# Packed 64-bit integer adds for GpSimd's tile shifts in a fused attention kernel

## Chip, cores, metric

One core of one Trainium2 chip. The metric is the device time of one execution in microseconds; a quoted time is the median of a kernel's runs. "Span" is the length of the one profiled execution, some 2 us less than a timed one. Ratios to the kernel before are the mean time of one kernel's fast runs over that of the other's of the same rounds, so not quite the ratio of the medians that are quoted.

## The reference

Two attention-like layers on separate inputs, whose outputs are put side by side. The change concerns the first, softmax attention with 32 heads of 16 over 2048 positions and one shared key and value head:

```python
def _A_ref(x, wq, wk, wv, wo):
    q = (x @ wq).reshape(B, S, 32, 16).transpose(0, 2, 1, 3)
    k = x @ wk
    v = x @ wv
    p = softmax(einsum("bhqd,bkd->bhqk", q, k) * 0.25)
    o = einsum("bhqk,bkd->bhqd", p, v)
    return o.transpose(0, 2, 1, 3).reshape(B, S, 512) @ wo
# B: linear attention with softmax feature maps, 32 heads; out = concat([A, B], -1)
```

## The kernel before

A Python scheduler inside the kernel plans the whole program with durations from its author (a "job" has an engine and a duration), and emits a fixed order for every engine. No order is decided at run time. The exponentials of the scores are shared out. ACT computes some with its Exp function into PT. DVE makes others: one linear map of a score tile to int16 (line 1743), whose bits, read as fp16, approximate an exponential. Four such tiles with bits offset by 0, 256, 512 and 768 form the terms of the approximation, and PE sums them with four scaled copies of V (VK, line 1811). A "quad" is four score tiles (128x2048) and its three offset copies; the ring Z has 12 slots of this size.

The offset copies, called shifts, are made by DVE or GpSimd ("pool"):

```python
def shifts(self, quad):
    ...
            if eng == "dve":
                fn = lambda v: v.tensor_scalar(out=Z[:, z], in0=Z[:, z0], scalar1=256.0 * t, ...)   # L1769
            else:
                a, b = (Z[:, x].rearrange("p h n -> p (h n)").bitcast(I32) for x in (z0, z))
                c = self.step[:, t - 2, :].bitcast(I32).to_broadcast([128, 1024])
                fn = lambda g: g.tensor_tensor(out=b, in0=a, in1=c, op=ALU.add)                     # L1774
    ...
    for t in (3, 2, 1):          # who makes shift t: GpSimd if its planned backlog allows
        left = max(self.te["pool"] - self.fin, 0.0) + self.PSHIFT * self.pooled
        eng = "pool" if t > 1 and left < self.PLEFT[3 - t] else "dve"
```

Shift 1 is always DVE's, and the program lets a GpSimd shift wait by semaphore for the DVE shifts of its own quad (cut from the code above: `deps=own`).

GpSimd also multiplies each of the first 31 of 32 finished accumulator blocks by the reciprocal of its denominators, and does small work for the linear attention:

```python
def finish_sc3(self, sc):        # L1879, 31 times
    self.add("pool", lambda v: v.tensor_tensor(out=o, in0=accS[:, r, :], in1=R[:, r, :], op=ALU.mult), ...)
def b_bm(self, st):              # L2080, 16 times, 128x64
    self.add("pool", lambda g: g.tensor_tensor(out=bmx, in0=ssum[:, r, :], in1=bmx, op=ALU.add), ...)
def b_kvfin(self):               # L2139 to L2144, once: 9 tensor_tensor, 1 tensor_scalar
```

## Time and profile before

| | before |
|---|---|
| time | 733.73 us (733.67 to 736.96, 3 runs) |
| PE, DVE, ACT, GpSimd busy, of a span of 731.1 us | 95%, 94%, 97%, 60% |
| shifts on GpSimd / DVE | 197 / 247 |
| mean GpSimd shift | 1893 ns |
| PE's wait for GpSimd's Z tiles | 1.5 us |

"Busy" is the time in which an engine executes something. ACT, PE and DVE are each close to full, so a gain has to lighten all three; GpSimd is the only one with room. The last row says that today its tiles are always ready in time. The lines themselves stand in the prediction.

### The profile page before, as it was taken

To read this page: it belongs to the slowest core of one execution; us is meant where nothing else is said; L and a number is where in the kernel's file an instruction comes from. 1 tells how busy PE (TensorE), PEld (TensorE's weight loads), DVE (VectorE), ACT (ScalarE), POOL (GpSimd) and SP (SyncE) were. 2 spreads that over 40 slices of the span, in tenths; PEclk is the share of its full clock that TensorE was granted. 3 is DMA by queue.
4 is the path that set the end of the run, shared out by engine and by line. 5 is a ranking of instruction groups with operands and counts; after the bars stand their busy time and mean duration, and the time that the engine had idled before them with its cause. 6 is when DMAs were issued, how large, how long until landed. Compare 5 with 4: busy or idle time off the path is not lost.

```text
span 731.1 us, 17986 instructions
## 1 busy us (share of the span) xinstructions
PE 693.6 (95%) x7450; PEld 215.9 (30%) x7450; DVE 686.1 (94%) x1157; ACT 709.5 (97%) x799; POOL 438.6 (60%) x307
## 2 busy tenths in 40 slices
PE   9999899999999999999999999999999999999995
PEld 3222222223222323322333323333333332332221
DVE  4899999999999999998999999999999999999991
ACT  5999999999999999999999999999999999999995
POOL 4474456666677566676346764455677556576553
PEclk9999999999999999999999999999999999999999
DMA  7620233111012110111101111101111012121002
GB/s 146 117 37 7 39 37 77 9 10 12 5 10 38 11 11 3 13 8 9 12 11 13 23 27 24 15 7 17 17 26 23 13 16 34 24 31 13 6 9 41
DMA packets 47890, 18.28 MB, mean 25 GB/s; under 512 B 38708, under 2 KB 45940, under 8 KB 47800
## 3 DMA queue, kind: packets, MB, share of 16 engines
q1 hardware_dynamic: 45400, 16.23, 17.5%
q8 instruction: 60, 0.98, 0.5%
q10 hardware_dynamic: 2400, 0.82, 0.5%
q14 instruction: 30, 0.25, 0.1%
HBM read 2.28 MB, written 4.19 MB: 9 GB/s over the span
## 4 chain that ended last, share of the span: by engine, by line
ACT 43%; PE 34%; DVE 19%; DMA 1%; POOL 1%; issue 0%; SPq 0%; ACTq 0%
ACT f_PT L1644 42%; PE f_ps L1589 12%; DVE f_Z L1743 10%; PE f_ps L1811 9%; DVE f_Z L1769 5%; PE f_ps L1685 4%; PE f_ps L2246 2%; PE f_ps L2154 1%; PE f_ps L1579 1%; PE f_ps L1898 1%; ACT f_Ek L2064 1%; DVE f_Wk L2216 1%; DMA f_AxT<-in_A_x_dram 1%; PE f_ps L2056 1%; PE f_ps L2230 1%; PE f_ps L2172 1%
## 5 line engine op out<-in xcount | busy, mean ns | idle before, releaser
L1644 ACT ACTIVATE f_PT<-f_ps 128x1024 bf16<-128x1024 f32 x728 | 680.7, 1076 | 11.8 <-PE f_ps L1589 10.8
L1774 POOL TENSOR_TENSOR f_Z<-f_Z,f_step 128x1024 int32<-128x1024 int32 x197 | 373.0, 1893 | 264.9 <-DVE f_Z L1769 258.9
L1743 DVE TENSOR_SCALAR f_Z<-f_ps 128x512 int16<-128x512 f32 x592 | 379.8, 679 | 13.0 <-PE f_ps L1589 11.7
L1589 PE MATMUL f_ps<-f_QA,f_KR 32*128 32x512 bf16 x2048 | 295.8, 384 | 21.1 <-ACT f_PT L1644 17.1
L1811 PE MATMUL f_ps<-f_Z,f_VK 128*32 128x512 f16 x2368 | 211.9, 386 | 5.7 <-POOL f_Z L1774 1.5
L1769 DVE TENSOR_SCALAR f_Z<-f_Z 128x2048 int16<-128x2048 int16 x247 | 168.0, 706 | 0.0
L1589 PEld LDWEIGHTS f_ps<-f_QA,f_KR 32*128 32x128 bf16 x2048 | 74.0, 91 | 260.9 <-ACT f_PT L1644 229.0
L1685 PE MATMUL f_ps<-f_PT,f_VA 128*32 128x512 bf16 x1456 | 137.4, 385 | 0.2
L1811 PEld LDWEIGHTS f_ps<-f_Z,f_VK 128*32 128x32 bf16 x2368 | 52.3, 93 | 109.2 <-issue 56.3
L1685 PEld LDWEIGHTS f_ps<-f_PT,f_VA 128*32 128x32 bf16 x1456 | 35.8, 94 | 49.1 <-issue 44.2
L1408 PE MATMUL f_ps<-f_ones,f_zero 128*128 128x512 bf16 (+5 forms) x182 | 34.5, 346 | 1.6 <-POOL f_zero L1427 1.3
L2216 DVE TENSOR_TENSOR f_Wk<-f_ps,f_wq 128x512 bf16<-128x512 f32 x32 | 21.8, 681 | 0.4 <-PE f_ps L2205 0.3
L1879 POOL TENSOR_TENSOR f_On<-f_accS,f_denS 128x512 bf16<-128x512 f32 x16 | 20.6, 1286 | 2.6 <-POOL f_Z L1774 0.4
L1414 DVE COPY f_accS<-f_ps 128x512 f32<-128x512 f32 x31 | 21.0, 679 | 0.0
L1879 POOL TENSOR_TENSOR f_Ot<-f_accS,f_denS 128x512 bf16<-128x512 f32 x15 | 19.0, 1269 | 3.1 <-DMA f_denS<-f_denS 1.3
L2104 DVE TENSOR_TENSOR f_vS<-f_ps,f_rs 128x1024 bf16<-128x1024 f32 x16 | 19.4, 1211 | 0.3 <-PE f_ps L2094 0.2
L2070 DVE TENSOR_REDUCE f_ssum<-f_Ek 128x64 f32<-128x1024 bf16 x16 | 19.2, 1200 | 0.0
L2064 ACT ACTIVATE f_Ek<-f_ps 128x512 bf16<-128x512 f32 x32 | 18.6, 681 | 0.0
L2161 ACT ACTIVATE f_ET<-f_ps 128x512 bf16<-128x512 f32 x32 | 18.5, 672 | 0.0
L2246 PE MATMUL f_ps<-f_Bwo,f_oT 128*128 128x512 bf16 x64 | 16.6, 382 | 0.6 <-DVE f_Z L1743 0.6
L1579 PE MATMUL f_ps<-f_AxT,f_wq 128*128 128x512 bf16 x64 | 16.4, 381 | 0.2 <-DVE f_Z L1743 0.2
L2094 PE MATMUL f_ps<-f_Bwv,f_BxT 128*128 128x512 bf16 x64 | 16.6, 382 | 0.0
(96 smaller groups left out, 303.1 us busy)
## 6 DMA issues: line engine op xcount, KB each, us to landing
f_denS<-f_denS SPq DMA_DIRECT2D x124, 30.0 KB, 3.1
out_dram<-f_outB SPq DMA_DIRECT2D x16, 128.0 KB, 1.9
f_denC<-f_accS SPq DMA_DIRECT2D x124, 2.0 KB, 1.7
f_denS<-f_denC SPq DMA_DIRECT2D x124, 2.0 KB, 1.7
out_dram<-f_outA SPq DMA_DIRECT2D x14, 128.0 KB, 1.9
f_On<-f_Ot SPq DMA_DIRECT2D x60, 16.0 KB, 1.8
f_Bwv<-in_B_wqkv_dram SPq DMA_DIRECT2D x1, 512.0 KB, 6.0
f_Bwo<-in_B_wo_dram SPq DMA_DIRECT2D x1, 512.0 KB, 4.5
```

Source lines behind the costliest of these rows:

```text
L1408: mm = pe.matmul(ps[m * i:m * i + m, bank, 0:n].rearrange("p (a n) -> p a n", n=128), lhsT=zero[0:r, 0:m], rhs=rhs, start=start, stop=star ...
L1589: return pe.matmul(self.ps[:, bank, :], lhsT=self.KR[32 * g:32 * g + 32, sc % 2, kap * 128:(kap + 1) * 128], rhs=self.QA[32 * g:32 * g + 3 ...
L1644: self.add("act", lambda a: a.activation(out=PT[:, sl[0]:sl[0] + size, :], in_=ps[:, b0:b0 + size, :], func=ACT.Exp), reads=[("PS", b0 + i ...
L1685: mm = pe.matmul(ps[32 * g:32 * g + 32, bank, :], lhsT=VA[:, kap, :], rhs=PT[:, slots[g], :], start=start, stop=stop, tile_position=(0, 32 ...
L1743: self.add("dve", lambda v: v.tensor_scalar(out=o, in0=ps[:, bank, :], scalar1=self.Z1, scalar2=self.Z0, op0=ALU.mult, op1=ALU.add), reads ...
L1769: fn = lambda v: v.tensor_scalar(out=Z[:, z], in0=Z[:, z0], scalar1=256.0 * t, scalar2=None, op0=ALU.add)
L1774: fn = lambda g: g.tensor_tensor(out=b, in0=a, in1=c, op=ALU.add)
L1811: mm = pe.matmul(ps[32 * g:32 * g + 32, bank, :], lhsT=self.VK[:, t, kap, :], rhs=Zf[:, sl[g], :], start=start, stop=stop, tile_position=( ...
L1879: self.add("pool", lambda v: v.tensor_tensor(out=o, in0=accS[:, r, :], in1=R[:, r, :], op=ALU.mult), reads=[("accS", r), ("denS", r), ("ro ...
L2064: self.add("act", (lambda a, sg: (lambda e: e.activation(out=Ek[:, r, a, :, :], in_=ps[:, bank, :].rearrange("p (h f) -> p h f", h=32), fu ...
L2216: self.add("dve", lambda v: v.tensor_tensor(out=o, in0=i, in1=w.unsqueeze(3).to_broadcast([128, 2, 16, 16]), op=ALU.mult), reads=[("PS", b ...
L2246: mm = pe.matmul(ps[:, bank, :], lhsT=oT[:, r, C, :], rhs=self.Bwo[:, C, :], start=(C == 0), stop=(C == 3))
```

## The change

The intent: an add of 32-bit words with a second input stream becomes an add of 64-bit words with an immediate, four int16 lanes a word (the bits are such that no lane overflows). One input stream in place of two should halve the time of a shift, and the scheduler, told 1.1 us in place of 1.97, should give GpSimd more of them.

```diff
+I64 = mybir.dt.int64
...
-                    a, b = (Z[:, x].rearrange("p h n -> p (h n)").bitcast(I32) for x in (z0, z))
-                    c = self.step[:, t - 2, :].bitcast(I32).to_broadcast([128, 1024])
-                    fn = lambda g: g.tensor_tensor(out=b, in0=a, in1=c, op=ALU.add)
+                    a, b = (Z[:, x].rearrange("p h n -> p (h n)").bitcast(I64) for x in (z0, z))
+                    fn = lambda g: g.int64_add(out=b, in0=a, in1=256 * t * 0x1000100010001)
...
-    PSHIFT = 1.97
+    PSHIFT = 1.1
```

## The prediction

> **What bounds the kernel now.** I read the page's first two parts first, to see whether any engine stands out. None does: three engines are near full, and GpSimd (POOL) is the one with room.
>
> ```profile
> PE 693.6 (95%) x7450; PEld 215.9 (30%) x7450; DVE 686.1 (94%) x1157; ACT 709.5 (97%) x799; POOL 438.6 (60%) x307
> ```
>
> Then the chain that ended last, by engine: it hops between ACT, PE and DVE all through the span, and GpSimd carries 1% of it.
>
> ```profile
> ACT 43%; PE 34%; DVE 19%; DMA 1%; POOL 1%; issue 0%; SPq 0%; ACTq 0%
> ```
>
> So the kernel is a balanced static schedule. It splits the attention scores between ACT (true exponentials) and DVE, which makes one fp16 bit pattern per score tile (line 1743). The other three tiles of a quad are that tile plus 256, 512 or 768: DVE and GpSimd make these "shifts". The costliest groups name all the pieces:
>
> ```profile
> L1644 ACT ACTIVATE f_PT<-f_ps 128x1024 bf16<-128x1024 f32 x728 | 680.7, 1076 | 11.8 <-PE f_ps L1589 10.8
> L1774 POOL TENSOR_TENSOR f_Z<-f_Z,f_step 128x1024 int32<-128x1024 int32 x197 | 373.0, 1893 | 264.9 <-DVE f_Z L1769 258.9
> L1743 DVE TENSOR_SCALAR f_Z<-f_ps 128x512 int16<-128x512 f32 x592 | 379.8, 679 | 13.0 <-PE f_ps L1589 11.7
> ...
> L1811 PE MATMUL f_ps<-f_Z,f_VK 128*32 128x512 f16 x2368 | 211.9, 386 | 5.7 <-POOL f_Z L1774 1.5
> L1769 DVE TENSOR_SCALAR f_Z<-f_Z 128x2048 int16<-128x2048 int16 x247 | 168.0, 706 | 0.0
> ...
> L1879 POOL TENSOR_TENSOR f_On<-f_accS,f_denS 128x512 bf16<-128x512 f32 x16 | 20.6, 1286 | 2.6 <-POOL f_Z L1774 0.4
> ```
>
> There are 592/4 = 148 quads, and 444 shifts: 247 on DVE, 197 on GpSimd. GpSimd's 264.9 us of idleness costs nothing today, because PE waits for its tiles only 1.5 us. Last I read the timeline of GpSimd, for the rhythm of its work:
>
> ```profile
> 50.23 3.86 POOL L1774 TENSOR_TENSOR f_Z<-f_Z,f_step 128x1024 int32<-128x1024 int32 x2 [1.10 <-DVE f_Z L1769]
> 54.23 1.53 POOL L1879 TENSOR_TENSOR f_On<-f_accS,f_denS 128x512 bf16<-128x512 f32 x1
> 56.52 1.89 POOL L1774 TENSOR_TENSOR f_Z<-f_Z,f_step 128x1024 int32<-128x1024 int32 x1 [0.75 <-DVE f_Z L1769]
> ```
>
> Shifts are broken by one floating-point multiply (line 1879) for each of 31 accumulator blocks. The first multiply starts at 54.2 us and the last at 719.0, so the rhythm is (719.0 - 54.2)/30 = 22.2 us a block, and 12.1 us follow the last one.
>
> **What the Trainium skill says.** "GPSIMD Engine Reference", section Performance versus the Vector engine: an add with two inputs is bound by two reads that take turns on one port, a body with at most two operations by about one cycle an element. The trace agrees: the two-input add of 1024 words takes 1893 ns, the fill of 1024 words of f_denS, with no input, 951 ns. The same page, section Instruction dispatch: GpSimd kernels are loadable libraries, and the first call after a load costs about 6 us (5.95 measured there), with no instruction visible in the profile. No view of the kernel before shows this cost: its fast path holds one library selection, of the library that is resident anyway, between the fills of f_half and the TENSOR_SCALAR after them, and the gap is an ordinary 0.09 us. "SBUF — State Buffer", section on the shared port pair: a DVE instruction in a 2-port mode and a GpSimd instruction exclude each other for their whole length. The 258.9 us that line 1774 waited for DVE's line 1769 fit this, mixed with plain data waits.
>
> **The change part by part.** I set the instruction order of the built kernel after against that of before.
>
> 1. The shift itself. One input stream and an immediate instead of two streams. Estimate: the kernel's constant went from 1.97 to 1.1 and the trace's spacing of two adjacent shifts is 3.86/2 = 1.93, so 1.1/1.97 x 1.93 = 1.08; the fill at 0.95 is a floor. I take 1.05 us.
>
> 2. The new split. The scheduler now believes in cheap GpSimd shifts: 310 shifts there (197 before), 158 on DVE (247), 156 quads (592 to 624 tiles of line 1743), 712 exponentials (728). DVE: +32 x 0.679 - 89 x 0.706 = -41 us. ACT: -16 x 680.7/728 = -15 us. PE: 128 more matmuls of line 1811, 32 fewer of line 1685, at about 0.09 us of busy time each (211.9/2368) some +8 us, partly taken back by fewer filler matmuls. If nothing else changed, ACT at 97% would set the end: 731 - 15 = 716 us in the profile, about 718 timed. That is the intended gain, 2%.
>
> 3. What the diff does not show. The 64-bit add is not in the resident library; the multiply of line 1879, the sum of line 2080 and other TENSOR_TENSOR are in it and not in the other. The build therefore puts a library selection in front of each change of kind. In the main path of the built kernel I count 40 in front of shifts, 28 in front of line 1879 and 12 in front of line 2080: 80 true changes, where there was none. At 6 us (the skill's figure, my estimate for both directions) that is 80 x 6 = 480 us of GpSimd time.
>
> 4. GpSimd's sum. 310 x 1.05 = 326, other work 438.6 - 373.0 = 66, loads 480: 872 us, against a span of 731. GpSimd becomes the bound.
>
> 5. By blocks, since the loads are not spread evenly. Of 31 blocks, 24 hold one pair of loads, 5 hold two and 2 hold three (the linear-attention part's small sums split them between 100 and 330 us). A block with one pair: 9.6 shifts x 1.05 + multiply 1.3 + 2 x 6 + small work 0.5 = 24 us, just above the rhythm of 22.2. Two pairs: 11 x 1.05 + 1.3 + 24 + 1 = 38. Three: 9.5 x 1.05 + 1.3 + 36 + 1.6 = 49. Sum: first block to its multiply 58 (54.2 and some), 23 x 24 = 552, 5 x 38 = 190, 2 x 49 = 98, tail 12: 910 us. PE, DVE and ACT follow, because the order on PE is fixed: a matmul of line 1811 whose tile is late stops all behind it. The Z ring has 12 slots, three quads, so while GpSimd loads for 6 to 13 us little can be made ahead, and after a load GpSimd sometimes waits for DVE in turn. I add 20 us for this: 930.
>
> **Rivals.** (a) The loads are cheap, under 0.5 us, or hidden in GpSimd's idle time. Without loads GpSimd would be busy 326 + 66 = 392 of about 716 us, so 80 loads of up to 324/80 = 4 us would fit on average. For it: the one selection in the trace of before costs nothing. Against it: that one selects the resident library, and idle time comes in pieces of 0.6 to 2.4 us in the timeline, so even 3 us would show at the small sums. Time: 716 to 735. (b) Loads cost 3.5 to 4 us: only the 7 blocks with several pairs are bound. With 4: 23 x 22.2 = 511, 5 x 30, 2 x 37, 70: 805, and 825 with the same allowance. (c) Loads cost 8 us or the add takes 1.5: with 8, 23 x 28 + 5 x 46 + 2 x 61 + 70 = 1066, or 1086 with the allowance; with a slow add, 310 x 0.45 = 140 us on top of 930. (d) The port becomes the bound: DVE's 158 shifts at 0.71 and GpSimd's 326 us exclude each other, 438 us of 731 against 168 + 373 = 541 before, so it eases; I drop it.
>
> **Range and chances.** The mechanism, a bound GpSimd, I hold for nearly sure; the size rests on the cost of a load, which no trace of before shows, at 80 us of span for each microsecond. A cost of 3.7 to 8.7 us gives about 800 to 1140 us, and I widen below for loads partly hidden. Predicted 930 us, 8 in 10 between 790 and 1140. Faster by over 2% needs loads of nearly nothing and all of the 2% gain: 0.05. Same: 0.06. Slower: 0.89.
>
> **What would show it.** Right: GpSimd shifts start to start about 1.05 us apart in runs of several; gaps of 5 to 7 us at each change between line 1774 and lines 1879 or 2080, put down to "issue" or to nothing; PE's waits at line 1811 for GpSimd's Z tiles from 1.5 us to over 100; slices between 100 and 330 us stretched most; PE, ACT and DVE down to 75% or so; ACT's time per exponential unchanged. Wrong: gaps at the changes under 1 us (rival a); shifts of 1.5 us or more; waits of PE for DVE or ACT in place of GpSimd; or a granted clock that falls as PE idles, which would add to my time.

## The result, and the profile after

1074.14 us (1068.88 to 1078.5, 4 runs), correct; the ratio to before is 1.462 (95% interval 1.454 to 1.470). The granted clock of PE fell from 0.998 to 0.824.

The page of the kernel after: its busy line, the slices of PE and of its clock, the chain that ended last by engine, and the groups that answer to those shown of before (count | busy us, mean ns | idle before them and its main releaser).

```profile
PE 767.0 (72%) x7468; PEld 218.2 (20%) x7526; DVE 674.0 (63%) x1100; ACT 711.4 (66%) x783; POOL 392.8 (37%) x420
...
PE   8976676676265778635746687888778877997676
...
PEclk9988876688686878666858898888888898898888
...
PE 33%; issue 27%; DVE 23%; POOL 10%; ACT 3%; DMA 1%; SPq 1%; POOLq 0%; ACTq 0%; DVEq 0%
...
L1645 ACT ACTIVATE f_PT<-f_ps 128x1024 bf16<-128x1024 f32 x712 | 681.1, 1049 | 341.5 <-PE f_ps L1590 338.8
...
L1774 POOL INT64_ADD f_Z<-f_Z x310 | 327.2, 1055 | 378.1 <-issue 186.4
L1811 PE MATMUL f_ps<-f_Z,f_VK 128*32 128x512 f16 x2496 | 251.6, 447 | 219.1 <-POOL f_Z L1774 217.8
...
L1879 POOL TENSOR_TENSOR f_On<-f_accS,f_denS 128x512 bf16<-128x512 f32 x16 | 20.6, 1286 | 111.0 <-issue 111.0
```

All four engines are less full than before, GpSimd's busy share too: 37% after 60%. An eye on busy shares alone would find no bottleneck here. The chain shows it: 27% of the span is "issue", time in which the engine on the chain waited for nothing that the profile shows. The shift itself is as fast as hoped, 1055 ns for 1893. But "issue" idle time now stands in front of the shifts (186.4 us) and of the multiplies (111.0 in this row, 84.4 in the other half of them), and PE's wait at line 1811 for GpSimd's tiles went from 1.5 us to 217.8.

What the "issue" time is, shows in the trace when one asks for everything that line 1879 and line 1774 put on GpSimd's queue. The first numbers are durations in ns (least, median, most):

```profile
L1879 POOLq MODIFY_POOL_CONFIG  x56: 11/11/12, 54.8 to 1050.1; - x56
...
L1774 POOLq MODIFY_POOL_CONFIG  x80: 1/1/13, 12.4 to 1034.2; - x80
```

Two records belong to one library selection: 28 in front of multiplies, 40 in front of shifts, and (24 records at line 2080) 12 in front of the small sum. That is the count of 80 which the prediction took from the built program. The records themselves last some nanoseconds; the time follows them. One change and its return, in the timeline of GpSimd (start, duration, operation, in brackets the idle time before it):

```profile
82.15 1.04 POOL L1774 INT64_ADD f_Z<-f_Z  x1 [1.30 <-DVE f_Z L1770]
90.58 1.26 POOL L1879 TENSOR_TENSOR f_Ot<-f_accS,f_denS 128x512 bf16<-128x512 f32 x1 [7.39 <-issue]
97.66 1.03 POOL L1774 INT64_ADD f_Z<-f_Z  x1 [5.83 <-issue]
98.86 1.04 POOL L1774 INT64_ADD f_Z<-f_Z  x1 [0.17 <-POOL f_Z L1774]
```

and the chain that ended last through the same 20 us, with PE after the long wait:

```profile
83.20 0.01 POOLq L1879
...
83.25 7.33 issue
90.58 1.26 POOL f_Ot L1879
...
92.08 5.59 issue
97.66 1.04 POOL f_Z L1774
98.70 0.04 issue
98.75 1.05 PE f_ps L1811 x8
```

GpSimd makes no tile from 83.19 to 97.66, 14.5 us for one multiply of 1.26. PE's eight matmuls at 98.75 had waited 7.9 us for the tile of 97.66. Before that it had run on with earlier tiles for 7.7 us, from 83.19 to 90.85; that first part of the outage was hidden. Over the trace, the gap in front of a return to the library of the multiplies is 6.92 us in the median (6.64 to 7.67, 40 gaps, 279.4 us), in front of a change to the 64-bit library 5.82 us (5.52 to 6.03, 39 gaps, 227.5 us; the 40th lay in idle time at the start). Together 506.8 us, 6.4 us a load. The profile puts 65 of the 79 gaps down to "issue"; the other 14 name DVE or PE but are as long.

### The profile page after: what moved, and what is told of

The parts are those of the page before. It is cut to its first block, busy times and chain, and to the rows that moved or that the text cites. A ratio compares the mean times of both kernels' runs of the same rounds, so it can differ in the third digit from the quotient of the medians.

```text
span 1070.3 us, 18343 instructions
## 1 busy us (share of the span) xinstructions
PE 767.0 (72%) x7468; PEld 218.2 (20%) x7526; DVE 674.0 (63%) x1100; ACT 711.4 (66%) x783; POOL 392.8 (37%) x420
## 4 chain that ended last, share of the span: by engine, by line
PE 33%; issue 27%; DVE 23%; POOL 10%; ACT 3%; DMA 1%; SPq 1%; POOLq 0%; ACTq 0%; DVEq 0%
DVE f_Z L1744 12%; PE f_ps L1590 11%; PE f_ps L1811 11%; POOL f_Z L1774 7%; PE f_ps L1686 5%; DVE f_Z L1770 4%; ACT f_PT L1645 3%; DVE f_vS L2104 1%; DVE f_Wk L2216 1%; POOL f_On L1879 1%; DVE f_ssum L2070 1%; DVE f_accS L1415 1%; PE f_ps L2154 1%; POOL f_Ot L1879 1%; PE f_ps L2094 1%
## 5 line engine op out<-in xcount | busy, mean ns | idle before, releaser
L1645 ACT ACTIVATE f_PT<-f_ps 128x1024 bf16<-128x1024 f32 x712 | 681.1, 1049 | 341.5 <-PE f_ps L1590 338.8
L1744 DVE TENSOR_SCALAR f_Z<-f_ps 128x512 int16<-128x512 f32 x624 | 409.7, 683 | 245.0 <-PE f_ps L1590 242.9
L1774 POOL INT64_ADD f_Z<-f_Z x310 | 327.2, 1055 | 378.1 <-issue 186.4
L1811 PE MATMUL f_ps<-f_Z,f_VK 128*32 128x512 f16 x2496 | 251.6, 447 | 219.1 <-POOL f_Z L1774 217.8
L1590 PE MATMUL f_ps<-f_QA,f_KR 32*128 32x512 bf16 x2048 | 312.8, 424 | 20.1 <-ACT f_PT L1645 11.8
L1686 PE MATMUL f_ps<-f_PT,f_VA 128*32 128x512 bf16 x1424 | 149.4, 424 | 0.1
L1770 DVE TENSOR_SCALAR f_Z<-f_Z 128x2048 int16<-128x2048 int16 x158 | 118.9, 754 | 1.9 <-PE f_ps L1811 0.7
L1879 POOL TENSOR_TENSOR f_On<-f_accS,f_denS 128x512 bf16<-128x512 f32 x16 | 20.6, 1286 | 111.0 <-issue 111.0
L1879 POOL TENSOR_TENSOR f_Ot<-f_accS,f_denS 128x512 bf16<-128x512 f32 x15 | 18.9, 1261 | 84.8 <-issue 84.4
L1409 PE MATMUL f_ps<-f_ones,f_zero 128*32 128x512 bf16 (+6 forms) x162 | 31.1, 383 | 1.6 <-POOL f_zero L1428 1.3
L1844 DVE RECIPROCAL f_denC<-f_denC 128x16 f32<-128x16 f32 x31 | 7.6, 244 | 35.9 <-DMA f_denC<-f_accS 35.9
L2117 PE MATMUL f_ps<-f_vS,f_Ek 128*32 128x34 bf16 x512 | 6.6, 186 | 30.3 <-POOL f_vS L2085 30.3
L2130 DVE TENSOR_TENSOR f_kvS<-f_ps,f_kvS 128x272 f32<-128x272 f32 x15 | 6.5, 437 | 22.7 <-PE f_ps L2117 22.6
```

The lines of the kernel that those rows point to most:

```text
L1409: mm = pe.matmul(ps[m * i:m * i + m, bank, 0:n].rearrange("p (a n) -> p a n", n=128), lhsT=zero[0:r, 0:m], rhs=rhs, start=start, stop=star ...
L1590: return pe.matmul(self.ps[:, bank, :], lhsT=self.KR[32 * g:32 * g + 32, sc % 2, kap * 128:(kap + 1) * 128], rhs=self.QA[32 * g:32 * g + 3 ...
L1645: self.add("act", lambda a: a.activation(out=PT[:, sl[0]:sl[0] + size, :], in_=ps[:, b0:b0 + size, :], func=ACT.Exp), reads=[("PS", b0 + i ...
L1686: mm = pe.matmul(ps[32 * g:32 * g + 32, bank, :], lhsT=VA[:, kap, :], rhs=PT[:, slots[g], :], start=start, stop=stop, tile_position=(0, 32 ...
L1744: self.add("dve", lambda v: v.tensor_scalar(out=o, in0=ps[:, bank, :], scalar1=self.Z1, scalar2=self.Z0, op0=ALU.mult, op1=ALU.add), reads ...
L1774: fn = lambda g: g.int64_add(out=b, in0=a, in1=256 * t * 0x1000100010001)
```

## The experiments

Three theories. **LT**: the loads make GpSimd's sum of work the bound; this is step 4 of the prediction, which its step 5 takes block by block. **LS**: every pair of loads is an outage that stalls the fixed order on PE by most of its length, whatever GpSimd's sum. **P**: not the loads but the 64-bit add or the new split does it, through the port that DVE and GpSimd share. Times of each experiment are beside runs of the kernel before on the same chip; its medians there were 733.56, 735.46 and 733.97 us in the three sessions.

### No library change, same order (a wrong result on purpose)

```diff
-  op of L1879: tensor_tensor(out=o, in0=accS[:, r, :], in1=R[:, r, :], op=ALU.mult)
+               tensor_copy(out=o, in_=accS[:, r, :])
-  op of L2080: tensor_tensor(out=bmx, in0=ssum[:, r, :], in1=bmx, op=ALU.add)
+               tensor_copy(out=bmx, in_=ssum[:, r, :])
```

> The changed kernel, instruction order untouched, but GpSimd's multiply (line 1879) and small sum (line 2080) made plain copies, which need no library: a wrong result on purpose. 2 library selections are left in front of shifts and 1 in front of the final small products, where there were 80. Theory L (the loads are the whole loss): 716 to 732 us, and about 718 plus one stall of up to 13 us. Theory P (the 64-bit add itself disturbs DVE through the shared port, or the new split is bad): stays above 900. Theory C (the lower PE clock is a cause of its own, not a result of the stalls): the clock stays near 0.82 and the time above 800; if L, the clock returns to about 1.0.

Measured: 734.72 us (733.47 to 735.34), ratio 0.9997 (0.9965 to 1.0028), clock 0.982; the result is wrong. With the order untouched and the same 310 adds, 339 us are gone:

```profile
L1774 POOL INT64_ADD f_Z<-f_Z x310 | 321.6, 1038 | 302.3 <-DVE f_Z L1770 265.0
L1811 PE MATMUL f_ps<-f_Z,f_VK 128*32 128x512 f16 x2496 | 213.5, 389 | 12.9 <-POOL f_Z L1774 11.3
```

P falls, and the low clock was a result of the stalls. (The copies are also shorter than the operations that they replace, 0.61 us for a multiply's 1.26; the run with loads alone, below, tests the loads from the other side.) But the intended 718 isn't reached either. The trace shows why: two changes of library are still on the path. The final small products need one pair, and ACT waits 11.3 us there. The other is at the head, ahead of ACT's first exponential:

```profile
16.28 1.94 ACT L1645 ACTIVATE f_PT<-f_ps 128x1024 bf16<-128x1024 f32 x2 [13.18 <-PE f_ps L1590]
364.54 1.02 ACT L1645 ACTIVATE f_PT<-f_ps 128x1024 bf16<-128x1024 f32 x1 [11.30 <-PE f_ps L1590]
```

and on GpSimd:

```profile
1.47 0.54 POOL L1442 MEMSET f_half<- 16x1 f32 x4
10.67 0.18 POOL L1444 TENSOR_SCALAR f_half<-f_half 128x1 f32<-128x1 f32 x1 [8.66 <-issue]
```

Same kernel, first 11 us of GpSimd. In the kernels before and after this gap is 0.10 and 0.32 us. Here the last GpSimd operation of an execution that needs one of the two libraries is a 64-bit add, so its library stays resident, and the next execution has to change it back first: 8.66 us. DVE's wait for its first keys grew from 7.2 to 13.7 us with it, and ACT's first exponential moved from 9.25 to 16.28 us. Without both, by subtraction, 734.7 - 11.3 - 7.0 = 716 us, an estimate that agrees with the intended gain; no run shows it.

### The old schedule with 64-bit adds

```diff
-    PSHIFT = 1.1
+    PSHIFT = 1.97
```

> The changed kernel with the schedule model's shift put back to 1.97, so the order is that of before with 197 64-bit adds and 88 loads (44 pairs). Two forms of theory L. LT (GpSimd's sum of work is the bound): 197 x 1.055 + 88 x 6.4 + 66 + 40 idle at the ends = 877 us. LS (each pair stalls the fixed order by a fixed amount, (1070 - 716)/40 = 8.9 us, whatever GpSimd's sum): 731 + 44 x 8.9 = 1120 us. Theory P: nearer to 731, as the add is shorter than before and there are no more of them.

Measured: 1149.56 us (1146.57 to 1150.36), ratio 1.564, correct. LS said 1120, LT 877. GpSimd is busy 24% of the span here and does less than in the kernel after, and yet the kernel is slower: there are 88 loads in place of 80, and ACT has 728 exponentials again in place of 712 (15 us).

```profile
L1774 POOL INT64_ADD f_Z<-f_Z x197 | 205.2, 1042 | 541.0 <-DVE f_Z L1770 281.3
```

LT falls as a bound by sum. It falls block by block too: the 19 blocks with one pair (the first block left out) hold 7.8 us of GpSimd's work and 12.8 us of loads, 20.6 us and so less than the rhythm of 22.2, and yet take 31.3 us on average. For 10.4 of them GpSimd waits for DVE.

### The small sum on DVE

```diff
-            job(("bm", st), "pool", 0.46, ...)
+            job(("bm", st), "dve", 0.16, ...)      # and its operation on DVE
-    LOCK = ("dS", "qw")
+    LOCK = ("dS", "qw", "bm")
```

> The changed kernel with only the small sum (line 2080) moved to DVE: 64 loads (32 pairs) in place of 80. LT: 312 x 1.055 + 64 x 6.4 + 61 + 40 = 840 us. LS: 716 + 32 x 8.9 = 1000 us. Theory P: no change, about 1070.

Measured: 963.86 us (960.17 to 966.95), ratio 1.312, correct. Eight pairs of loads fewer took away 110 us, nearly 14 us each, the whole length of an outage. LS said 1000, LT 840: nearer to LS, though a single figure a pair is too simple. The pairs taken away were those that followed each other closely.

### Loads alone, in the kernel before

```diff
+        self.add("pool", lambda v: v.int64_add(out=tick, in0=tick, in1=1), reads=["tick"], writes=["tick"])  # 16 words
         self.add("pool", lambda v: v.tensor_tensor(out=o, in0=accS[:, r, :], in1=R[:, r, :], op=ALU.mult), ...)
```

> The kernel before, 32-bit shifts and its schedule, with one 64-bit add of 16 words put ahead of each of the 31 multiplies: 62 loads and nothing else of the change. LT: 439 + 62 x 6.4 + 40 = 876 us. LS: 731 + 31 x 8.9 = 1007 us. Theory P: 731 to 740, since there is no 64-bit add of a Z tile.

Measured: 1120.01 us (1114.15 to 1120.74, 3 fast runs; a fourth, 1131.06, is slow), ratio 1.530, correct. LS said 1007, LT 876, P 740 at most: all too low, LS by the least. No shift was changed, and 62 loads alone cost 386 us, 12.5 us a pair. The timeline of GpSimd in this run:

```profile
89.87 0.19 POOL L1883 INT64_ADD f_tick<-f_tick  x1 [5.69 <-issue]
97.14 1.25 POOL L1884 TENSOR_TENSOR f_Ot<-f_accS,f_denS 128x512 bf16<-128x512 f32 x1 [7.08 <-issue]
98.53 3.93 POOL L1777 TENSOR_TENSOR f_Z<-f_Z,f_step 128x1024 int32<-128x1024 int32 x2
```

An add of 0.19 us costs 13 us of GpSimd. The gaps have the same lengths as in the kernel after (medians 5.75 and 6.96), so they belong to the change of library and not to the size of the tile. Here more of an outage reaches the end than in the old schedule with fast shifts (9.5 us a pair there, 416 us over 44). That a backlog is worked off more slowly at 1.93 us a shift than at 1.2 is a likely reason, but only argued.

### One more pair at each multiply

```diff
+        self.add("pool", ... tensor_tensor(out=t32, in0=t32, in1=t32, op=ALU.add) ...)   # 16 words
+        self.add("pool", ... int64_add(out=t64, in0=t64, in1=1) ...)                     # 8 words
         self.add("pool", ... tensor_tensor(out=o, in0=accS[:, r, :], in1=R[:, r, :], op=ALU.mult), ...)
```

> The changed kernel with one more change of library and back ahead of each of the 31 multiplies (two tiny operations): 142 loads in place of 80. If the fixed order hides a first part of every outage and nothing after it, each added pair costs its whole length: 1074 + 31 x (12.8 + 0.3) = 1480 us. If stalls stay at the 9 us a pair seen so far: 1074 + 31 x 8.9 = 1350 us.

Measured: 1492.23 us (1489.1 to 1497.14), ratio 2.031, correct. The first form was right: 418 us for 31 added pairs, 13.5 us each, the length of a pair with its tiny operations. The order hides a first part of an outage and nothing of what is added to it. The page of this run has PE waiting at its Z matmuls for GpSimd for 526.0 us, after 217.8.

### The scheduler told of the loads

```diff
-            job(("on", sc), "pool", 1.16, ...)
+            job(("on", sc), "pool", 1.16 + 12.8, ...)
-            job(("bm", st), "pool", 0.46, ...)
+            job(("bm", st), "pool", 0.46 + 12.8, ...)
```

> The changed kernel, but the schedule model is told that each multiply and each small sum keeps GpSimd for 12.8 us more. The scheduler then gives GpSimd only 102 shifts (33 changes into the 64-bit library, 33 out) and DVE 336. If the loss comes from a fixed order that did not foresee the loads: 740 to 790 us with 66 loads still there. If loads cost their 9 us a pair whatever the order: 733 + 33 x 8.9 = 1027 us.

Measured: 963.49 us (959.62 to 967.99), ratio 1.310, correct. Neither expectation held. (These two jobs were also taken out of the model's lock on the shared port, and the flag that guards a fallback path is read at the very end of each engine's program.) PE's wait for GpSimd's tiles is down to 14.4 us, so the scheduler did plan around the outages. It lost the time elsewhere: ACT idles 130 us in front of exponentials (11.8 in the kernel before), and the last exponential ends at 842.6 us. The linear attention, whose small sums now cost GpSimd 13 us each in the plan, gets its final small products at 845 us (329 in the kernel before), and runs on alone for about 107 us. So a model that knows of the loads doesn't rescue this layout. How a better order would do with 66 loads stays open.

### All other library work on DVE

```diff
-            job(("on", sc), "pool", 1.16, ...)       # multiply
+            job(("on", sc), "dve", 0.62, ...)
-            job(("bm", st), "pool", 0.46, ...)       # small sum
+            job(("bm", st), "dve", 0.16, ...)
-        self.job("kvfin", "pool", 5.0, ...)          # final small products
+        self.job("kvfin", "dve", 2.0, ...)
-    LOCK = ("dS", "qw")
+    LOCK = ("dS", "qw", "on", "bm")
```

> The changed kernel with everything on GpSimd that needs the other library after the start (multiply, small sum, final small products) moved to DVE, results correct. One load in the steady path, one at the head, because the execution before left the 64-bit library resident (8.7 us of idle ahead of line 1444 in the copy experiment). The built order has 306 GpSimd shifts, 153 DVE shifts, 718 exponentials. Theory L: 733.6 - (728 - 718) x 0.935 = 724, plus some 6 us at the head = 724 to 731 us. If work on DVE takes back all: 733 to 745.

Measured: 729.48 us (727.47 to 731.48, 6 runs), ratio 0.9909 (0.9878 to 0.9941), correct. The change and the work moved to DVE give 0.9% together, clear of noise but small, with the load at the head still there (8.6 us of idle in front of line 1444).

### The same move with the old add

The same diff on the kernel before; the fallback flag is read at the end here too.

> Control for the last: the kernel before (32-bit two-input shifts) with the same work moved to DVE, no loads at all (the read of the fallback flag stands at the very end of each engine's program, as the check wanted). 207 GpSimd shifts, 234 DVE shifts, 730 exponentials. If the 64-bit add itself is worth something: slower than the last run's kernel by 730 - 718 = 12 exponentials or 11 us: 735 to 745 us. If the move to DVE alone is the gain: the same as the last run's kernel.

Measured: 761.27 us (760.01 to 768.77, 6 runs), ratio 1.0354 (1.0309 to 1.0399), correct. Moving the work to DVE costs time by itself; with the 64-bit add it pays. Of the 32 us between the two runs some 8 lie at the end: 18.8 us follow the last exponential here, 10.6 in the last run. In this order the small sums slipped behind the last exponentials on DVE, and they and the flag that is computed from them (743.8 to 750.3 us) stand ahead of the last block's work. The remaining 24 or so are what the shorter shift is worth in this layout, by subtraction and not by a run of its own.

### No second library at all

```diff
-        add("pool", lambda e: e.tensor_scalar(out=half[:, 1:2], ...))
+        add("dve", lambda e: e.tensor_scalar(out=half[:, 1:2], ...))
+            add("pool", lambda g: g.int64_add(out=tick, in0=tick, in1=1), ...)   # ahead of affine_select, which follows it in the trace after 0.08 us
-                    add("pool", ... tensor_scalar(out=mask[rows, a, j:j + 1], ...))
+                    add("dve", ... tensor_scalar(out=mask[rows, a, j:j + 1], ...))
```

> The kernel with the work on DVE, and the head's few GpSimd operations that need the other library put on DVE too, so no execution after the first changes the library. Theory L: 5 to 8 us less than the kernel without this, 717 to 725 us; ratio to before 0.977 to 0.99. If the head's load was hidden: no difference.

Measured: 727.89 us (726.81 to 735.22, 6 runs), ratio 0.9912 (0.9868 to 0.9957): no difference to the last but one can be told. The 8.6 us gap is gone (the first 64-bit add, behind a selection of its own, waits 0.14 us), but DVE's instructions for the mask now wait 7.1 us for GpSimd's fill of the mask, with the keys of the first scores behind them in DVE's order. ACT's first exponential moved from 17.0 to 12.2 us only; before it was 9.25.

```diff
+        add("dve", ... tensor_scalar(out=self.half4, in0=half, scalar1=4.0, ...))       # early, 128x2
-                    add("dve", ... tensor_scalar(out=mask[rows, a, j:j + 1], ...))
+                    add("pool", ... tensor_copy(out=mask[rows, a, j:j + 1], in_=self.half4[rows, a:a + 1]))
```

> The version with the work on DVE and no second library, with the mask's scaling done once on DVE early and copied by GpSimd, so that DVE's first instruction for the keys isn't held by it (in the run before ACT's first exponential began at 12.2 us against 9.25 in the kernel before). Expected 3 us less: 724 to 725 us. If the head is not on the path: 728.

Measured: 726.13 us (724.09 to 728.65, 6 runs), ratio 0.9876 (0.9838 to 0.9914), correct. ACT starts at 9.60 us. Near the expected 725, but the intervals of this ratio and of the last overlap. ACT starts 7.4 us earlier than in the run with the load at the head; the medians differ by 3.4 us, measured in different sessions.

### More quads on DVE

```diff
-    AHEAD = 6
+    AHEAD = 4        # and, in another run, 3
```

> The same with AHEAD at 4: 714 exponentials, 155 quads. ACT bound: 4 x 0.935 = 3.7 us less than the version with 718, about 721 us. If PE or DVE has become the bound: no gain.

> The same with the scheduler's AHEAD at 3 in place of 6, which lets it give DVE more quads: 710 exponentials (718), 157 quads (153). ACT bound: 8 x 0.935 = 7.5 us less, 717 us, 0.976 of before. If PE or DVE has become the bound: no gain, 724 or more.

Measured: with 4, 722.14 us (719.85 to 725.02, 6 runs), ratio 0.9827 (0.9789 to 0.9865); with 3, **715.56 us** (713.56 to 716.85, 6 runs), ratio 0.9732 (0.9698 to 0.9766), both correct. The last beats both kernels; at 2% it is the only run that counts as faster. Its page:

```profile
PE 672.8 (94%) x7451; PEld 213.5 (30%) x7512; DVE 675.7 (95%) x1162; ACT 693.0 (97%) x781; POOL 342.3 (48%) x368
...
ACT 41%; PE 34%; DVE 20%; issue 1%; DMA 1%; SPq 1%; POOL 0%; POOLq 0%; ACTq 0%
...
L1779 POOL INT64_ADD f_Z<-f_Z x314 | 325.9, 1038 | 344.4 <-DVE f_Z L1775 324.6
```

"Issue" is back at 1% of the chain, the three engines are balanced as in the kernel before, and GpSimd does 314 shifts in less busy time than 197 took before. Whether AHEAD at 3 would also help the kernel before was not run, so how much of the 2.7% is the 64-bit add's stays open.

## Why the prediction was right, and where its size was off

- **Direction and cause: right.** Slower, by library selections that the diff doesn't show. It counted 80 in the built program; the trace has 160 records, two a selection. Taking nearly all loads away, with order and adds kept, brought 1074 back to 735, and loads alone took the kernel before to 1120.
- **Step 1, the shift: right.** 1.05 us taken, 1.055 measured. In backlog the start-to-start spacing is 1.13 us, or 1.21 where GpSimd waits 0.17 us for its own semaphore; 1.05 was expected there.
- **Step 2, the intended gain: supported, not shown.** About 718 timed without loads was predicted; 734.7 was measured with two load delays left, some 716 by subtraction. The kernels without loads have other work on DVE.
- **Step 3, the load: nearly right.** 6 us taken for both directions; 5.82 one way, 6.92 back, 6.4 on average.
- **Step 4, GpSimd's sum: right as a sum, wrong as the bound.** 872 predicted; 392.8 busy and 506.8 of loads are 900. GpSimd was idle for about 170 us of the span on top, some 122 of them for DVE's line 1770 (15.5 before its first shift).
- **Step 5, the blocks: this is the step that failed in size.** A block with one pair was to take its own GpSimd work, 24 us; the 23 after the first took 28.9 on average. Two pairs: 38 predicted, 45 measured; three: 49 and 53. With 62 for the first block and 13 at the end this gives the 1070 of the span: 23 x 28.9 + 5 x 45 + 2 x 53 + 75. The trace takes a single-pair block apart: 11.9 us of GpSimd's work, as predicted; 12.9 of loads, where 12 were taken; and 4.1 of waiting, where none was taken (3.1 for DVE, 0.9 for its own semaphore). What failed is the form of the sum. The prediction took the larger of GpSimd's work with loads and the rhythm of 22.2 us, as if PE, DVE and GpSimd could make up for an outage in each other's idle time, and added 20 us for where they can't. The old schedule with 64-bit adds shows best that they can't: 20.6 us of work and loads there, below the rhythm, made blocks of 31.3. The order is fixed and the engines feed each other: while GpSimd is out, PE stops (after 7.7 us in the outage shown), DVE stops with it for want of scores, and after the load GpSimd finds only a few tiles ready and waits for DVE in turn. So much of an outage is added to the rhythm: of 12.8 us a pair, 8.9 reached the end here, 9.5 in the old schedule, 12.5 with loads alone. The 20 us term would have had to be about 130: the span exceeds the 910 us of the blocks by 160, of which the longer loads explain some 30.
- **Luck in the range.** It was made wide for the unknown cost of a load. The load came out near the guess; what was missed lay in the allowance, for which no range was given. Rival (c), loads of 8 us, comes closer with 1086, but by a cause that the trace rules out.
- **What was to show it: right**, with one addition. The waits of PE, the gaps put down to "issue" and the unchanged exponential (1049 ns, 1076 before) were there. PE, DVE and ACT fell lower (72, 63 and 66%) than the 75% expected. The falling clock, named as something that would add to the time, came: 0.824. A matmul of line 1811 took 447 ns after 386. How much of the span the slower clock itself makes was not separated; no run here has the stalls without it. An estimate of the most is 79 us, as PE was busy 767.0 us here and 687.9 with the same order in the copy run.
- **Rivals.** (a), cheap or hidden loads: refuted. (b) and (c), other sizes of the load: neither, as the load was near 6. (d), the port: the copy experiment has the same adds beside DVE's shifts and runs at 735, so it isn't the bound. The 258.9 us of waiting for line 1769, which the prediction reads as fitting the port's exclusion, are semaphore waits for an order that the program sets and say nothing of the port.

## What to carry to other kernels

Look at the built program for what an operation brings along, not only at the diff: an instruction from another GpSimd library costs a load each time the work changes hands, here 13 us a pair, and the profile shows it mostly as idle time put down to "issue" behind records of some nanoseconds. When one engine of a fixed, balanced order is taken out for longer than the others have work queued, count most of the outage onto the critical path (8.9 to 12.5 us of 12.8 a pair in these runs), not only into that engine's sum of busy time. If a fast operation lives in another library, move everything else on that engine into operations that both libraries or none need, down to the head of the program; then rebalance.

## What the Trainium skill lacked or had wrong

- "GPSIMD Engine Reference", section Instruction dispatch, gives about 6 us (5.95) for the first call after a library load. The runs agree for the way into the 64-bit library (5.82 us in the median, 5.52 to 6.03) and show that every later change costs it again. The way back takes longer, 6.92 us (6.64 to 7.67); the page gives one figure for any library.
- The same section says that no visible instruction shows the load, and measures it from a MODIFY_POOL_CONFIG record on. The trace agrees: a selection has two such records on GpSimd's queue, of 1 to 13 ns, and the load's time is no instruction's. The page lacks that a selection of the library that is resident already leaves the same records and costs nothing (gaps of 0.10 to 0.32 us).
- No page read has that the library stays resident from one execution to the next: the two kernels whose last operation of either library is a 64-bit add and whose first is not paid 8.66 and 8.56 us at their own head, where the others paid 0.1 to 0.3. Why this is more than 6.92 is not shown.
- No page read tells which operations share a library, or that the build puts selections in. Here multiply and sum of two tensors on one side and the 64-bit add on the other needed 80, while copies needed none.
- "GPSIMD Engine Reference", section Performance versus the Vector engine, puts an add with two inputs at about 2.6 cycles an element, and its section Instruction dispatch the floor at about 2.5. 1893 ns for 1024 words at the page's 1.2 GHz are 2.2 cycles, an estimate; the second input here is one word repeated. The multiply of line 1879, with two full inputs of 512 words, takes 1261 to 1286 ns, 3.0 cycles, so the page's floor is not shown to be wrong for such inputs. The page's section When to use GPSIMD notes that the two-tensor add is refused on 64-bit tiles; the 64-bit add with an immediate used here is another operation, 1.04 to 1.06 us for 512 such words, and the page doesn't have it.
